# Banded attention and a gated MLP in one kernel: the late attention two units at a time, in thirteen visits instead of thirty-six

## The chip, the cores and the metric

One core of a Trainium2 chip runs one program. The metric is the time of the program on the device in microseconds, the median of several runs. The engines are TensorE (PE; PEld is its weight load), VectorE (DVE), ScalarE (ACT), GpSimd (POOL) and SyncE (SP, which issues most DMAs).

## The reference

Attention over 4 batches and 8 heads of 768 positions with 64 elements each. The positions fall into 24 chunks of 32. A chunk's queries see 8 memory tokens, 16 positions to the left, the chunk itself and 8 positions to the right. The result, 3072 tokens of 512, goes through an RMS norm and a gated MLP with 1536 hidden elements:

```
k_full = concat(mem_k, k[chunk - 16 : chunk + 40]);  v_full likewise
scores = q_c @ k_full.T / 8;  a = exp(scores - max);  a = a / (sum(a) + 1e-9)
x = a @ v_full                               # per chunk and head, then (3072, 512)
xn = x / sqrt(mean(x*x) + 1e-6) * rms_g
g = xn @ w_gate;  out = (silu(g) * (xn @ w_val)) @ w_out
```

## The kernel before, in words

All is fp32. In the MLP each operand is split into a high and a low part, and each product is made of three matmuls (high·high, low·high, high·low: `PASS`).

**Work units.** The tokens fall into 8 blocks of 384. A block's attention is four units, one for each pair of heads, so there are 32 units; units 0 to 7 (blocks 0 and 1) are made early, units 8 to 31 late. A unit goes through these steps: `load_qk` (8 DMA issues, L165 and L167) and `load_v` (a copy of the memory values on ScalarE, L227, and DMAs, L211); `stage_t` (L287 and L292: transposes of q and k on VectorE, with two copies on ScalarE); `stage_s` (L318, s: 12 matmuls, shown as 24); `stage_m` (L330, L336: maximum and subtraction on VectorE) and `stage_e` (L341, exp on ScalarE); `stage_p` (L348, pT: three transposes on TensorE); `stage_c` (L227 and L230: a copy of pT's upper half on ScalarE and of its lower half on VectorE); `stage_o` (L368, o); `stage_r` (L382 to L391: division on VectorE, into x). The late units before share one set of buffers: q and pT in one tile (tag A), k and v in another (tag B), and qn, kn, single too, for the untransposed loads.

**MLP of a block.** For each of 12 slices f of the hidden layer, TensorE makes a gate group pg and a value group pv (L561, 12 matmuls each, PSUM banks "g" and "v"), and an output group po (L599, 9 matmuls) of the slice before; ScalarE and VectorE make hh and hl between them (tanh L568, L572, L575, cast L227, L584). `split_x` between two blocks transposes the normed x (xT, L440) and makes its high and low parts xh, xl (L445, L450). `finish` (from L611, po L627) is the last slice of the last block.

**Order.** Blocks 0 and 1, with the preparation of the weights, stand in the string `ORDER`, a row of tokens, each one step of a unit, of the weights or of the MLP; its instructions are issued in that order. The rest is a loop over seven segments (L857): slices 5 to 11 of block 0, then blocks 2 to 7. In segment n the attention of block n + 2 is made in visits, as long as there is one. A segment has two gaps for each slice, numbered from 0: an even one behind pg, an odd one behind pv and ahead of po. A visit at a gap puts its steps there (`visit`, L870). TensorE's instructions keep the program's order (`on_pe`); those of the other engines are placed by a scheduler, with the visits at a higher priority. `attn_visits` (L688) has six visits of a block on TensorE: s | pT s | pT s o | pT s o | pT o | o, where each piece is of another unit, and a seventh for the norm (`stage_n`: squares on ScalarE, L398; the root on GpSimd, L412; the scaling, L419 and L421). The gaps are `FIRST` in the first segment and are spread out evenly in the others.

Of the kernel before, what the change touches and what calls it, by code (L numbers as in the profile page):

```python
# [19 lines left out]
CH = 32  # L20
# [3 lines left out]
P = 128  # L24
# [43 lines left out]
def tile_kernel(ctx: ExitStack, tc: tile.TileContext, q, k, v, mem_k, mem_v,  # L68
# [48 lines left out]
    NE = NG * 2  # L117
    late_kv = {}
    KW, VW = (NC + 1) * KC, NJ * 2 * (D + 1)

    def late_attention():

        t = p1.tile([P, NKT * HT], F32, name="qp", tag="A")
        n = NC * 2 * CH
        qbs[0] = t[:, 0:n].rearrange("p (c s q) -> p c s q", c=NC, s=2)
        pts[0] = t[:, n:].rearrange("p (i a s q) -> p i a s q", i=NT, a=4, s=2)
        nc.vector.memset(t, 0.0)
        t = p1.tile([P, KW + VW], F32, name="kv", tag="B")
        late_kv["kw"] = t[:, 0:KW].rearrange("p (c k) -> p c k", k=KC)
        late_kv["vw"] = t[:, KW:].rearrange("p (j h d) -> p j h d", j=NJ, h=2)  # L130
    units = [(b, hf, g) for b in range(B) for hf in range(2) for g in range(NG)]
    st = {}

    def which(u):

        return 1 + u % 2 if u < NE else 0

    def unit_tile(u, shape, tag, n):

        if u < NE:  # L140
            return early.tile(shape, F32, name=f"{tag}{u}", tag=f"{tag}{u % n}")
        if tag in late_kv:
            return late_kv[tag]
        return p1.tile(shape, F32, name=f"{tag}{u}", tag=tag)
# [123 lines left out]
    def stage_q0(u, e="a"):  # L268
        d = st[u]
        qb = qbs[which(u)]  # L270
# [12 lines left out]
    def stage_ta(u):  # L283
        d = st[u]
        qb = qbs[which(u)]
        for hh in range(2):
            nc.vector.transpose(out=qb[64 * hh:64 * hh + 64, :, hh, :], in_=d["q"][64 * hh:64 * hh + 64])  # L287
# [21 lines left out]
    def stage_s(u):  # L309
        d = st[u]  # L310
        qb = qbs[which(u)]
        s = psum_a(f"s{u}")
# [29 lines left out]

    def stage_p(u):
        d = st[u]
        t = psum_a(f"pT{u}") if u >= NG else psum_m("o0", f"pT{u}")
        pe = d["p"].rearrange("p j k -> p (j k)")
        for i in range(NT):
            on_pe(nc.tensor.transpose(out=t[:, i * P:(i + 1) * P], in_=pe[:, i * P:(i + 1) * P], identity=ident))  # L348
        d["t"] = t
# [5 lines left out]
    def stage_ch(u, hh, e):  # L355
        r = slice(64 * hh, 64 * hh + 64)
        t4 = st[u]["t"][:, 0:HT].rearrange("p (i a q) -> p i a q", i=NT, q=CH)
        copy(e, pts[which(u)][r, :, :, hh, :], t4[r])

    def stage_o(u):  # L360
        d = st[u]
        pt = pts[which(u)]
        o = psum_a(f"o{u}") if u >= NG else psum_m(f"o{1 + u % 2}", f"o{u}")
        for i in range(NT):
# [44 lines left out]
    def stage_ny(ss):  # L409
        sr = p2.tile([P, NT], F32, name="sr", tag="sr")  # L410
        nc.vector.scalar_tensor_tensor(out=sr, in0=ss[:, 0], scalar=DM * 1e-6, in1=ss[:, 1], op0=ALU.add, op1=ALU.add)
# [275 lines left out]

    def attn_visits(blk, x):  # L688


        us = list(range(blk * NG, (blk + 1) * NG))
        for n in range(NG + 2):
            with tc.high_priority():
                if 1 <= n <= NG:
                    stage_p(us[n - 1])
                if n < NG:
                    u = us[n]
                    stage_s(u)
# [12 lines left out]
            if n < NG and u + 2 < len(units):
                load_qk(u + 2)
            yield
        with tc.high_priority():
            stage_n(x)
        yield

# [74 lines left out]
    def tok_o(n):  # L792
# [62 lines left out]
    xs = xs01[0]  # L855
    nxt = 2
    for sg, (blk, f0) in enumerate(segments):  # L857
        po = [psm_o(i) for i in range(NT)] if sg else sp["po", 0]
        todo = iter(())
        if nxt < NBLK:  # L860
            x = new_x()
            todo = attn_visits(nxt, x)
            nxt += 1
        last = sg == len(segments) - 1
        gaps = 2 * (NF - f0)
        when = [n * (gaps - GAPS) // (NG + 1) for n in range(NG + 2)] + [gaps - GAPS + 1]
        if sg == 0:
            when = FIRST
# [60 lines left out]
```

## Time and profile before

| what | value |
|---|---|
| time, median of 3 runs | 732.41 us (731.84 to 733.12) |
| span of the profiled execution | 729.8 us |
| instructions | 13052 |
| TensorE busy | 715.1 us, 5136 instructions |
| VectorE, ScalarE, GpSimd busy | 380.0, 287.8, 36.4 us |
| moved by DMA | 50.20 MB |

The span is the time of the profiled execution from its first to its last instruction; the program's time is some 2.6 us longer than this span. A row of the timeline gives the start in the span, the duration, engine, line and operation, what is written and read, the shapes and the count, and in brackets how long the engine was idle just ahead and which instruction ended that. Rows of the same kind in succession are drawn together (x24); their duration is that of all together.

### The profile page before, as it was taken

The page shows a single profiled execution, that of the slowest core. Times are in us where ns is not written, and L with a number is a line of the kernel's source. Part 1 is how long each engine was busy: PE and PEld are TensorE (multiplying, and loading weights), DVE is VectorE, ACT ScalarE, POOL GpSimd, SP SyncE. Part 2 cuts the span into 40 slices and gives each one's busy share as a digit, 9 for nine tenths or more (in the row PEclk, how much of TensorE's full clock was granted, in tenths as well). Part 3 has the DMA queues.
Part 4 walks back from the last instruction along what each step waited for, and adds up shares of the span by engine and source line. Part 5 has one row for each costly group of instructions (what it writes and reads, how often), then busy time and mean ns, then how long its engine had stood idle before and what let it go on. Part 6 is the DMA issues. An engine that isn't in the chain of part 4 may idle for free.

```text
span 729.8 us, 13052 instructions
## 1 busy us (share of the span) xinstructions
PE 715.1 (98%) x5136; PEld 656.6 (90%) x5136; DVE 380.0 (52%) x725; ACT 287.8 (39%) x600; POOL 36.4 (5%) x143
## 2 busy tenths in 40 slices
PE   8889999999999999999999999999999999999997
PEld 7778999999989999899999999989998999999996
DVE  4888999865645443444535353445434543332222
ACT  4899676643452323422333232432234222341112
POOL 3300000001000000000000000000000000000000
PEclk8999999999999999999999999999999999999999
DMA  8994563414412320122212123021311210010001
GB/s 173 203 259 141 173 202 116 132 37 102 85 37 68 55 50 22 62 46 42 43 38 66 23 45 61 20 66 31 66 29 34 64 32 20 20 44 0 1 1 43
DMA packets 143173, 50.20 MB, mean 69 GB/s; under 512 B 126984, under 2 KB 134536, under 8 KB 143112
## 3 DMA queue, kind: packets, MB, share of 16 engines
q1 hardware_dynamic: 139832, 44.49, 26.6%
q10 hardware_dynamic: 3280, 4.88, 1.8%
q8 instruction: 40, 0.66, 0.4%
q14 instruction: 21, 0.17, 0.1%
HBM read 43.06 MB, written 6.29 MB: 68 GB/s over the span
## 4 chain that ended last, share of the span: by engine, by line
PE 92%; ACT 3%; DMA 3%; DVE 1%; issue 0%; POOL 0%; ACTq 0%; SPq 0%; POOLq 0%
PE pv L561 28%; PE po L599 28%; PE pg L561 27%; PE s L318 3%; PE o L368 3%; PE xT L440 1%; PE pT L348 1%; DMA ws<-in_moe_w_val_dram 1%; DMA memV<-in_mem_v_dram 1%; DMA vw<-in_v_dram 1%; ACT junk L398 0%; ACT ws L508 0%; ACT pt L227 0%; DMA kv<-in_v_dram 0%; ACT qb L227 0%
## 5 line engine op out<-in xcount | busy, mean ns | idle before, releaser
L561 PE MATMUL pv<-xh,wh_v 128*128 128x384 f32 x384 | 132.8, 346 | 0.0
L561 PE MATMUL pg<-xh,wh_g 128*128 128x384 f32 x384 | 129.7, 338 | 0.7 <-DVE t L572 0.7
L561 PE MATMUL pv<-xh,wl_v 128*128 128x384 f32 x384 | 129.5, 337 | 0.6 <-DVE wl_v L532 0.6
L561 PE MATMUL pg<-xh,wl_g 128*128 128x384 f32 x384 | 129.5, 337 | 0.0
L561 PE MATMUL pg<-xl,wh_g 128*128 128x384 f32 x384 | 129.3, 337 | 0.0
L561 PE MATMUL pv<-xl,wh_v 128*128 128x384 f32 x384 | 129.3, 337 | 0.0
L572 DVE SCALAR_TENSOR_TENSOR t<-t,pg 128x384 f32<-128x384 f32 x96 | 53.1, 553 | 138.6 <-ACT t L568 138.5
L227 ACT CAST hh<-t 128x384 fp32r<-128x384 f32 x95 | 48.7, 512 | 174.9 <-PE po L599 165.3
L599 PE MATMUL po<-wh_o,hh 128*128 128x512 f32 x285 | 113.8, 399 | 0.3
L599 PE MATMUL po<-wh_o,hl 128*128 128x512 f32 x285 | 113.1, 397 | 0.0
L599 PE MATMUL po<-wl_o,hh 128*128 128x512 f32 x285 | 112.1, 393 | 0.0
L584 DVE TENSOR_TENSOR hl<-t,hh 128x384 fp32r<-128x384 f32 x95 | 52.9, 557 | 100.7 <-ACT hh L227 95.7
L568 ACT ACTIVATE t<-pg 128x384 f32<-128x384 f32 x96 | 47.2, 492 | 135.9 <-PE pg L561 130.8
L575 DVE TENSOR_TENSOR t<-t,pv 128x384 f32<-128x384 f32 x95 | 52.5, 552 | 64.9 <-PE pv L561 64.4
L561 PEld LDWEIGHTS pg<-xh,wh_g 128*128 128x128 f32 x384 | 72.1, 188 | 4.4 <-DVE t L572 0.9
L561 PEld LDWEIGHTS pg<-xl,wh_g 128*128 128x128 f32 x384 | 72.1, 188 | 3.6
L561 PEld LDWEIGHTS pv<-xh,wh_v 128*128 128x128 f32 x384 | 72.1, 188 | 2.4
L561 PEld LDWEIGHTS pv<-xh,wl_v 128*128 128x128 f32 x384 | 72.2, 188 | 0.9 <-DVE wl_v L532 0.9
L561 PEld LDWEIGHTS pv<-xl,wh_v 128*128 128x128 f32 x384 | 72.2, 188 | 0.3
L561 PEld LDWEIGHTS pg<-xh,wl_g 128*128 128x128 f32 x384 | 72.1, 188 | 0.0
L599 PEld LDWEIGHTS po<-wh_o,hl 128*128 128x128 f32 x285 | 53.5, 188 | 14.1 <-DVE hl L584 1.8
L599 PEld LDWEIGHTS po<-wh_o,hh 128*128 128x128 f32 x285 | 53.5, 188 | 10.0 <-ACT hh L227 1.7
(112 smaller groups left out, 772.9 us busy)
## 6 DMA issues: line engine op xcount, KB each, us to landing
kn<-in_k_dram SPq DMA_DIRECT2D x96, 52.0 KB
qn<-in_q_dram SPq DMA_DIRECT2D x96, 48.0 KB
out_dram<-ob ACTq DMA_DIRECT2D x18, 256.0 KB
ws<-in_moe_w_gate_dram SPq DMA_DIRECT2D x4, 1024.0 KB
ws<-in_moe_w_val_dram SPq DMA_DIRECT2D x4, 1024.0 KB
ws<-in_moe_w_out_dram SPq DMA_DIRECT2D x4, 1024.0 KB
kv<-in_v_dram SPq DMA_DIRECT2D x48, 84.0 KB
kv<-in_v_dram SPq DMA_DIRECT2D x48, 70.0 KB
```

The lines of the kernel that those rows point to most:

```text
L227: return nc.scalar.copy(out, in_)
L318: on_pe(nc.tensor.matmul(s[64 * par:64 * par + 64, o:o + KC], lhsT=qb[:, c].rearrange("p s q -> p (s q)"), rhs=kw[:, c], start=True, stop= ...
L348: on_pe(nc.tensor.transpose(out=t[:, i * P:(i + 1) * P], in_=pe[:, i * P:(i + 1) * P], identity=ident))
L368: on_pe(nc.tensor.matmul(o[64 * par:64 * par + 64, c0:c0 + D + 1], lhsT=pt[:, i, 2 * par + hh].rearrange("p c q -> p (c q)"), rhs=d["v"][: ...
L440: on_pe(nc.tensor.transpose(out=t[:, i * P:(i + 1) * P], in_=tiles[i][:, kt * P:(kt + 1) * P], identity=ident))
L561: on_pe(nc.tensor.matmul(ps[:, 0:HT], lhsT=weight(a, n, f, kt), rhs=xs[c][:, kt], start=cnt == 0, stop=cnt == 3 * NKT - 1))
L568: nc.scalar.activation(t, g, AF.Tanh, scale=0.5)
L572: nc.vector.scalar_tensor_tensor(out=t, in0=t, scalar=1.0, in1=g, op0=ALU.add, op1=ALU.mult)
L575: nc.vector.tensor_tensor(out=t, in0=t, in1=vv, op=ALU.mult)
L584: nc.vector.tensor_tensor(out=hl, in0=t, in1=hh.bitcast(F32), op=ALU.subtract)
L599: on_pe(nc.tensor.matmul(po[i], lhsT=h[a][:, i * P:(i + 1) * P], rhs=weight(c, "o", f), start=f == 0 and n == 0, stop=f == NF - 1 and n == 2))
```

## The change

**Late attention in pairs.** `late_steps` takes the place of `attn_visits`. It goes over the twelve pairs of late units in one generator for all blocks. A full visit on TensorE is pT pT of the pair before, s s of this pair, o o of the pair before, and ends with "v". There are 13: one with s s alone, eleven full ones, and the last in two parts, pT pT ("p") and o o. A table `VISITS` says for each segment at which gap which step comes: "v", "n" (the norm), and "t" (the transposes of q and k of the pair's second unit; those of its first come with the visit). Transposes of a pair are put behind the last VectorE instruction issued so far (`behind_last`). In a pair both units' V are loaded in the visit of their s.

**Banks.** In a visit the first pT goes into the gate bank "g", the second o into the value bank "v" (not in the last visit), and the rest into the three banks of `psa`.

**Buffers.** Each unit of a pair has its own set: the odd ones the old ones (A and B), the even ones new tiles in the space that the staging of the weights leaves (tags "qb", "ws" and "wy"). qn and kn stay single, so the loads of a unit start when those of the unit before are transposed.

**The first late unit in `ORDER`.** New tokens R0 to R4: R0 loads q and k of unit 8, R1 makes its buffers (a memset of qb1), R2 transposes it, R3 makes pt1 (a memset), R4 loads its V and q and k of unit 9.

**The end.** In `finish` hh and hl take tags A and B instead of "hh" and "hl".

**Places.** The tiles `zero` and `first` move to the early pool, `ss` and `sr` to the single one. The lines before and after in what follows: pT L348 and L377, s L318 and L346, o L368 and L398, pg and pv L561 and L591, po L599 and L629, xT L440 and L470, the transposes L287/L292 and L315/L320, copies L227/L230 and L255/L258.

```diff
+VISITS = (((1, "v"), (4, "t"), (5, "v"), (8, "t"), (11, "v"), (12, "n")),
+          ((2, "t"), (5, "v"), (8, "t"), (17, "v"), (18, "n"), (20, "t")),
+          ((5, "v"), (8, "t"), (17, "v"), (18, "n"), (20, "t")),
+          ((5, "v"), (8, "t"), (17, "p"), (18, "v"), (19, "n")))
...
-j13 F g14 k13a I l13 Ha L Z J o13 f h14 F I v14 i14 Ha L g15 j14 Z J k14a f l14 F v15 h15 I i15 Ha
-g16 j15 J L f F o14 I Ha L v16 k15a l15 h16 o15 i16 j16
+j13 F g14 k13a I l13 Ha L Z J o13 f h14 F I v14 i14 Ha L g15 j14 Z R0 J k14a f l14 F v15 h15 I i15 R1 Ha
+g16 j15 J L R2 R4 f F o14 I Ha R3 L v16 k15a l15 h16 o15 i16 j16
...
-    def stage_p(u):
+    def stage_p(u, tag=None):
         d = st[u]
-        t = psum_a(f"pT{u}") if u >= NG else psum_m("o0", f"pT{u}")
+        tag = tag or (None if u >= NG else "o0")
+        t = psum_m(tag, f"pT{u}") if tag else psum_a(f"pT{u}")
...
-        hh = p1.tile([P, HT], F32R, name="hh", tag="hh")
-        hl = p1.tile([P, HT], F32R, name="hl", tag="hl")
+        hh = p1.tile([P, HT], F32R, name="hh", tag="A")
+        hl = p1.tile([P, HT], F32R, name="hl", tag="B")
...
+    def behind_last(u):
+        done = next(i for i in reversed(nc.cur_bb.bb.instructions) if i.engine == nc.vector.engine)
+        with tc.issue_after(done):
+            stage_t(u)
+
+    def late_steps():
+
+
+        pairs = [(u, u + 1) for u in range(NE, len(units), 2)]
+        for n in range(len(pairs) + 1):
+            old = pairs[n - 1] if n else ()
+            cur = pairs[n] if n < len(pairs) else ()
+            new = pairs[n + 1] if n + 1 < len(pairs) else ()
+            for u in old[0:1]:
+                if u % NG == 0:
+                    late_x["x"] = new_x()
+            x = late_x.get("x")
             with tc.high_priority():
-                if 1 <= n <= NG:
-                    stage_p(us[n - 1])
-                if n < NG:
-                    u = us[n]
+                for i, u in enumerate(old):
+                    stage_p(u, None if i else "g")
+                for u in old:
+                    stage_c(u)
+            if not cur:
+                yield "p"
+            with tc.high_priority():
+                for u in cur:
                     stage_s(u)
...
+                for u in cur:
                     stage_m(u)
+                for u in cur:
                     stage_e(u)
...
+                for i, u in enumerate(old):
+                    stage_o(u, "v" if cur and i else None)
+                for u in old:
+                    stage_r(u, x)
+                for u in new[0:1]:
+                    behind_last(u)
+            for u in new[0:1]:
+                load_qk(u + 1)
+            for u in cur if n else ():
+                load_v(u)
+            yield "v"
+            if n and n % 2 == 0:
+                with tc.high_priority():
+                    stage_n(x)
+                yield "n"
+            if new:
+                with tc.high_priority():
+                    behind_last(new[1])
+                if n + 2 < len(pairs):
+                    load_qk(pairs[n + 2][0])
+            yield "t"
...
+        if n == 0:
+            load_qk(NE)
+        if n == 1:
+            late_buffers(1)
+        if n == 2:
+            stage_t(NE)
+        if n == 3:
+            late_pt()
+        if n == 4:
+            load_v(NE)
+            load_qk(NE + 1)
```

TensorE in a visit of block 4 (units 16 to 18), before: the end of a gate group, one piece of each kind, and the start of the value group.

```order
L561 MATMUL pg_3689<-xh_3391,wl_g2_94 128x384
L348 MATMUL pT17_3702<-ident_99,pe17_3593 128x128 x3
L318 MATMUL s18_3706<-kv_1946,qp_1944 64x64 x12
L368 MATMUL o16_3719<-kv_1946,qp_1944 64x65 x12
L561 MATMUL pv_3768<-xh_3391,wh_v2_95 128x384
```

After, units 16 to 19 in a full visit between a value group and an output group:

```order
L591 MATMUL pv_3634<-xh_3488,wl_v1_90 128x384
L377 MATMUL pT16_3648<-ident_99,kv1_1882 128x128 x3
L377 MATMUL pT17_3652<-ident_99,pe17_3246 128x128 x3
L346 MATMUL s18_3660<-kv1_1882,qb1_1880 64x64 x12
L346 MATMUL s19_3673<-kv0_1978,qp0_1976 64x64 x12
L398 MATMUL o16_3695<-kv1_1882,pt1_1942 64x65 x12
L398 MATMUL o17_3708<-kv0_1978,qp0_1976 64x65 x12
L629 MATMUL po0_3541<-wh_o1_91,hh_3617 128x512
```

The visit has moved from behind pg to behind pv and holds two units of each kind, next to each other.

VectorE in the first segment, before, around the copy of the first late pT (pT8; qn and kn are the loaded q and k, t the gate's product):

```order
L584 TENSOR_TENSOR hl_2065<-t_2059,hh_2063 128x384
L292 STREAM_TRANSPOSE kv_1946<-kn9_1965 128x13x32
L336 TENSOR_TENSOR pe8_2038<-s8_2023,mx8_2036 128x384
L572 SCALAR_TENSOR_TENSOR t_2144<-t_2144,pg_2067 128x384
L575 TENSOR_TENSOR t_2144<-t_2144,pv_2080 128x384
L230 COPY qp_1944<-pT8_2093 64x12x32
```

After, at the same copy:

```order
L614 TENSOR_TENSOR hl_2154<-t_2148,hh_2152 128x384
L315 STREAM_TRANSPOSE qp0_1976<-qn11_2095 64x12x32 x2
L320 STREAM_TRANSPOSE kv0_1978<-kn11_2096 128x13x32
L602 SCALAR_TENSOR_TENSOR t_2322<-t_2322,pg_2156 128x384
L605 TENSOR_TENSOR t_2322<-t_2322,pv_2187 128x384
L258 COPY pt1_1942<-pT8_2201 64x12x32
L258 COPY qp0_1976<-pT9_2205 64x12x32
L358 TENSOR_REDUCE mx10_2239<-s10_2213 128x6
```

By then units 9 to 11 are transposed where it was unit 9 alone, and the transposes of unit 11 stand directly ahead of the read of pg.

ScalarE in the first segment, before, around the norm of block 2 (memV are the memory values, junk and ss the squares, sr the root), up to the first xh:

```order
L568 ACTIVATE t_2516<-pg_2442 128x384
L398 ACTIVATE junk_2493,ss_2492<-x_1978 128x384 x3
L227 COPY kv_1946<-memV_102 128x12x64
L398 ACTIVATE junk_2497,ss_2492<-x_1978 128x128 x3
L419 ACTIVATE x_1978<-x_1978,sr_2501 128x512
L227 CAST hh_2520<-t_2516 128x384
L568 ACTIVATE t_2550<-pg_2524 128x384
L445 ACTIVATE xh_2558<-xT0_2560,rg_100 128x384
```

After:

```order
L255 COPY kv0_1978<-memV_102 128x12x64
L428 ACTIVATE junk_2602,ss_2601<-x_2200 128x384 x2
L428 ACTIVATE junk_2606,ss_2601<-x_2200 128x128
L255 CAST hh_2584<-t_2580 128x384
L428 ACTIVATE junk_2602,ss_2601<-x_2200 128x384
L428 ACTIVATE junk_2606,ss_2601<-x_2200 128x128
L328 COPY kv1_1882<-kv1_1882 128x12x16
L329 COPY kv1_1882<-kv1_1882 128x11x8
L428 ACTIVATE junk_2606,ss_2601<-x_2200 128x128
L598 ACTIVATE t_2629<-pg_2588 128x384
L449 ACTIVATE x_2200<-x_2200,sr_2610 128x512
L475 ACTIVATE xh_2637<-xT0_2639,rg_100 128x384
```

The squares now stand behind both copies of memory values and among copies of the next block's k; fewer MLP steps lie between the scaling and the first xh.

More of the change, by code (lines that the diff above doesn't have):

```diff
@@ L117, in tile_kernel, with late_buffers, late_pt, late_views @@
     NE = NG * 2
-    late_kv = {}
+    late = {}
     KW, VW = (NC + 1) * KC, NJ * 2 * (D + 1)
[L121 to L130, printed above, removed]
+    NQ = NC * 2 * CH
+    def late_buffers(i):
+        if i:
+            late["qb", 1] = p1.tile([P, NQ], F32, name="qb1", tag="qb")
+            nc.vector.memset(late["qb", 1], 0.0)
+        else:
+            t = p1.tile([P, NKT * HT], F32, name="qp0", tag="A")
+            late["qb", 0], late["pt", 0] = t[:, 0:NQ], t[:, NQ:]
+            nc.vector.memset(t, 0.0)
+        t = p1.tile([P, KW + VW + i * NJ * KC], F32, name=f"kv{i}", tag=("B", "ws")[i])
+        late["kw", i] = t[:, 0:KW].rearrange("p (c k) -> p c k", k=KC)
+        late["vw", i] = t[:, KW:KW + VW].rearrange("p (j h d) -> p j h d", j=NJ, h=2)
+        if i:
+            late["pe", i] = t[:, KW + VW:].rearrange("p (j k) -> p j k", k=KC)
+        else:
+            late_views("pt", i)
+        late_views("qb", i)
+    def late_pt():
+        late["pt", 1] = p1.tile([P, NQ], F32, name="pt1", tag="wy")
+        nc.vector.memset(late["pt", 1], 0.0)
+        late_views("pt", 1)
+    def late_views(n, i):
+        if n == "qb":
+            late[n, i] = late[n, i].rearrange("p (c s q) -> p c s q", c=NC, s=2)
+        else:
+            late[n, i] = late[n, i].rearrange("p (i a s q) -> p i a s q", i=NT, a=4, s=2)
     units = [(b, hf, g) for b in range(B) for hf in range(2) for g in range(NG)]
     st = {}
-    def which(u):
-        return 1 + u % 2 if u < NE else 0
+    def qb_of(u):
+        return qbs[1 + u % 2] if u < NE else late["qb", 1 - u % 2]
+    def pt_of(u):
+        return pts[1 + u % 2] if u < NE else late["pt", 1 - u % 2]
     def unit_tile(u, shape, tag, n):
@@ L269, in stage_q0 @@
         d = st[u]
-        qb = qbs[which(u)]
+        qb = qb_of(u)
         q4 = split4(d["tq"], HT)
@@ L284, in stage_ta @@
         d = st[u]
-        qb = qbs[which(u)]
+        qb = qb_of(u)
         for hh in range(2):
@@ L310, in stage_s @@
         d = st[u]
-        qb = qbs[which(u)]
+        qb = qb_of(u)
         s = psum_a(f"s{u}")
@@ L357, in stage_ch, with stage_o @@
         t4 = st[u]["t"][:, 0:HT].rearrange("p (i a q) -> p i a q", i=NT, q=CH)
-        copy(e, pts[which(u)][r, :, :, hh, :], t4[r])
-    def stage_o(u):
+        copy(e, pt_of(u)[r, :, :, hh, :], t4[r])
+    def stage_o(u, tag=None):
         d = st[u]
-        pt = pts[which(u)]
-        o = psum_a(f"o{u}") if u >= NG else psum_m(f"o{1 + u % 2}", f"o{u}")
+        pt = pt_of(u)
+        tag = tag or (None if u >= NG else f"o{1 + u % 2}")
+        o = psum_m(tag, f"o{u}") if tag else psum_a(f"o{u}")
         for i in range(NT):
@@ L711, in attn_visits @@
[L711 to L716, printed above, removed]
+                for i, u in enumerate(old):
[8 more added lines that the diff above has]
+                load_v(u)
@@ L855, in tile_kernel @@
     xs = xs01[0]
-    nxt = 2
+    todo = late_steps()
     for sg, (blk, f0) in enumerate(segments):
         po = [psm_o(i) for i in range(NT)] if sg else sp["po", 0]
[L859 to L863, printed above, removed]
         last = sg == len(segments) - 1
[L865 to L868, printed above, removed]
+        steps = {} if last else dict(VISITS[min(sg, 2) + (sg == len(segments) - 2)])
         def visit(gap):
-            for _ in range(when.count(gap)):
-                next(todo, None)
+            if gap in steps and next(todo, None) not in (steps[gap], None):
+                raise AssertionError(gap)
         for f in range(f0, NF):
```

44 lines of the change are left out of this document (14 added, 30 removed).

## The prediction

> **What bounds the kernel now.** I read the totals first, then the busy table by stretches, then the timeline of TensorE around single visits, then the waits that end idle time on TensorE. The totals and the page's row on TensorE:
>
> ```profile
> span 729.8 us, 13052 instructions
> PE 715.1 (98%) x5136; PEld 656.6 (90%) x5136; DVE 380.0 (52%) x725; ACT 287.8 (39%) x600; POOL 36.4 (5%) x143
> ```
>
> TensorE is busy 715.1 of 729.8 us, every other engine half as long or less. So the change can gain where TensorE does less or waits less, and lose where it waits anew. The next rows put a segment with attention beside the last one, which has none; both run from the first gate matmul to the point where the last 10 of 12 output groups lie behind (12 pg, 12 pv and 10 po groups). Columns: stretch, us, busy time of PE, PEld, DVE, ACT and POOL, granted TensorE clock, DMA share, GB/s.
>
> ```profile
> 563.81:644.13 80.32, 80.32 (x584) 74.60 (x583) 34.21 (x70) 22.98 (x55) 2.66 (x10) 1.00 0.15 34
> 650.07:721.20 71.13, 71.13 (x379) 67.17 (x378) 18.89 (x34) 12.24 (x25) 0.00 (x0) 1.00 0.03 12
> ```
>
> TensorE has no gap in either (80.32 of 80.32, 71.13 of 71.13). The attention of one block of four units therefore costs 80.32 − 71.13 = 9.19 us of TensorE, and six late blocks cost 55.1 us. The 205 instructions more are, but for one, 4 × (3 pT + 24 s + 24 o). The instructions stay the same; only what the switches between kinds of work cost can fall.
>
> **Part by part. 1: the pieces merge (−8.1).** TensorE's timeline of a visit with s alone, of one with three pieces, and the row of nine transposes of x (start, us, instruction, shapes, count):
>
> ```profile
> 220.70 0.34 PE L561 MATMUL pg<-xh,wl_g 128*128 128x384 f32 x1
> 220.97 0.97 PE L318 MATMUL s<-kv,qp 128*64 128x64 f32 x24
> 221.86 0.45 PE L561 MATMUL pv<-xh,wh_v 128*128 128x384 f32 x1
> ...
> 246.18 0.34 PE L561 MATMUL pg<-xh,wl_g 128*128 128x384 f32 x1
> 246.36 0.49 PE L348 MATMUL pT<-ident,pe 128*128 128x128 f32 x3
> 246.78 0.97 PE L318 MATMUL s<-kv,qp 128*64 128x64 f32 x24
> 247.53 0.92 PE L368 MATMUL o<-kv,qp 128*64 128x65 f32 x24
> 248.38 0.44 PE L561 MATMUL pv<-xh,wh_v 128*128 128x384 f32 x1
> 248.66 0.34 PE L561 MATMUL pv<-xl,wh_v 128*128 128x384 f32 x1
> ...
> 644.13 1.14 PE L440 MATMUL xT<-ident,x 128*128 128x128 f32 x9
> ```
>
> From start to start, pT takes 0.42, s before an o 0.75, s before a large matmul 0.89, o 0.85. The first large matmul behind a visit takes 0.28 (248.38 to 248.66) where one beside its like takes 0.18 (246.18 to 246.36): 0.10. An s that follows a large matmul pays about 0.09 at its entry (0.27 from 220.70 to 220.97), and I take 0.07 for an o alone. Before, the six visits of a block are s | pT s | pT s o | pT s o | pT o | o: 0.98 + 1.31 + 2.02 + 2.02 + 1.27 + 0.92, and six times 0.10, is 9.1: it accounts for the 9.19.
>
> After, TensorE has thirteen visits: one s s, eleven of pT pT s s o o, and the last as pT pT and o o one gap apart. Three transposes more behind the first three cost 3 × 0.108 (nine span 1.14 and three 0.49: 0.65 for six), so pT pT 0.74. Two s cost 1.49 (2 × 0.745). For the first o of two no row shows the switch; its 24 matmuls leave 0.85 less the 0.14 by which s before a large matmul exceeds s before an o, so 0.71, and o o takes 1.55. With 0.10 behind it a full visit is 3.88; eleven are 42.7. The first visit is 0.09 + 1.64 + 0.10 = 1.8, the last 0.74 and 1.75. Together 47.0 against 55.1: **−8.1**. The bounds: if a switch to the second piece of a kind cost as much as to another kind, a visit would be 2 × 0.42 + 2 × 0.75 + 2 × 0.85 + 0.10 = 4.14, 2.9 more in eleven; below, the pair of transposes could be 0.66 and the second s 0.70, 1.4 less.
>
> **2: the first block's wait goes (−1.15).**
>
> ```profile
> 203.22 1.26 PE L368 MATMUL o<-kv,qp 128*64 128x65 f32 x24 [0.80 <-DMA kv<-in_v_dram]
> 204.42 0.44 PE L561 MATMUL pv<-xh,wh_v 128*128 128x384 f32 x1
> ```
>
> The last o of block 2 waits 0.80 for its values and then runs 1.20 instead of 0.85. After, the values of a pair are loaded in the visit that computes its s, and are used in the next visit, four gaps or more away, some 3 us each (the segment of 80.32 us has 24). Nothing is late next at this place; what is late a little behind it is step 4.
>
> **3: the end (−0.4).**
>
> ```profile
> 721.20 0.40 PE L599 MATMUL po<-wh_o,hh 128*128 128x512 f32 x1
> ...
> 723.06 0.40 PE L599 MATMUL po<-wh_o,hl 128*128 128x512 f32 x1
> 723.61 0.50 PE L627 MATMUL po<-wh_o,hh 128*128 128x512 f32 x1 [0.15 <-ACT hh L621]
> 723.26 0.70 ACT L621 CAST hh<-t 128x128 fp32r<-128x128 f32 x3 [3.46 <-PE po L599]
> ```
>
> The last hh is cast only when the po group ahead has read the old hh (3.46 of waiting), so the last group starts 0.55 behind the matmul ahead instead of (723.06 − 721.20) / 8 = 0.23, and its first matmul is 0.1 longer. With hh and hl in buffers that are free by then the cast runs beside that po group: −0.4.
>
> **4: the norm of block 2 gets tight (+1.4).** The rows of that norm before:
>
> ```profile
> 202.85 0.49 ACT L398 ACTIVATE junk<-x 128x384 f32<-128x384 f32 x1
> 203.48 0.49 ACT L398 ACTIVATE junk<-x 128x384 f32<-128x384 f32 x1
> 204.66 0.82 ACT L227 COPY kv<-memV 128x768 f32<-128x768 f32 x1
> 205.55 0.28 ACT L398 ACTIVATE junk<-x 128x128 f32<-128x128 f32 x1
> 205.99 0.28 ACT L398 ACTIVATE junk<-x 128x128 f32<-128x128 f32 x1
> 207.28 0.15 DVE L411 SCALAR_TENSOR_TENSOR sr<-ss 128x3 f32<-128x3 f32 x1
> 208.40 0.72 ACT L419 ACTIVATE x<-x,sr 128x512 f32<-128x512 f32 x1 [1.57 <-POOL sr L412]
> ```
>
> Before, the squares of three of the four head pairs stood ahead of the last o. After, the visit at gap 11 brings the last two units of the block, and all six squares stand behind it on ScalarE, behind two copies of pT, two exps and two copies of memV. From the visit's start T0: o o ends at 3.9, the second memV copy (0.82) at about 5.4; the squares take 3 × 0.63 + 3 × 0.44 = 3.2, and a hh cast and two kv copies of 0.95 in all stand among them: 9.5. Then 0.1, 1.12 to the root (207.28 to 208.40) and 0.9 for scaling three tiles on two engines: 11.6. TensorE reaches xT after the visit (3.9), a po (9 × 0.23), pg and pv (12 × 0.174 each, from the two stretches' 71.13): 10.2. It waits 11.6 − 10.2 = **1.4**, bounds 0.9 and 1.9 by half a us in the order on ScalarE. The other five norms have five gaps or more of TensorE work behind them, some 15 us, and cost nothing; without that cover each would cost the like.
>
> **5: transposes on VectorE that wait for a DMA (+0.2).** Each pair has two transposes on VectorE (q and k), and the second unit's load can only start when the first's is transposed. Around gap 5 of block 0 those of unit 11 stand ahead of t<-t,pg (L572), which frees the gate bank that the next pT, lent that bank, now needs: the first pT and all of TensorE behind it would wait.
>
> ```profile
> 173.04 0.47 SPq L167 DMA_DIRECT2D kn<-in_k_dram  x1
> 176.59 0.61 DVE L292 STREAM_TRANSPOSE kv<-kn 128x416 f32<-128x416 f32 x1 [0.57 <-DMA kn<-in_k_dram]
> 188.66 0.47 SPq L167 DMA_DIRECT2D kn<-in_k_dram  x1
> 191.40 0.61 DVE L292 STREAM_TRANSPOSE kv<-kn 128x416 f32<-128x416 f32 x1
> ```
>
> From the last issue of a load to its transpose lie 3.55 us where it waited and at most 2.74 where it did not. The loads of units 9, 10 and 11 hang on each other through one buffer, so the difference of 0.8 counts up to three times: a wait of 2.3, or none. I take 0.2, near the unwaited row, since of these two landings one only was waited for. The Trainium skill's "DMA: Bandwidth & Descriptors" (Anatomy of one DMA) puts the fixed part of a transfer at about 2 us, under both rows; by it the wait would be nothing and the time 0.2 lower, and no run here shows the fixed part alone.
>
> **6: block 0 and 1's end (+0.15).** Into the row of tokens go two memsets and a unit's transposes on VectorE:
>
> ```profile
> 1.57 0.70 DVE L656 MEMSET qb<- 128x768 f32 x1
> 156.88 0.56 DVE L584 TENSOR_TENSOR hl<-t,hh 128x384 fp32r<-128x384 f32 x1 [0.27 <-ACT hh L227]
> 158.91 0.40 PE L599 MATMUL po<-wh_o,hl 128*128 128x512 f32 x1
> 248.26 1.17 DVE L287 STREAM_TRANSPOSE qp<-qn 64x384 f32<-64x384 f32 x2
> ```
>
> The hl shown ends at 157.44 and is first read at 158.91: 1.5 of room. Ahead of it now stand 0.70 + 1.17 + 0.61 = 2.5 of new work, of which I estimate that 1 us falls into VectorE's idle time: it then starts at 158.4, ends at 158.96 and is read some 0.1 later. **+0.15**, bounds 0 and 0.5 (no idle time at all would cost 1 us, but 0.27 of it stands in the row itself and more ahead). The same memset and transposes leave the place behind, where TensorE did not wait for them.
>
> **What stays covered.** In a full visit VectorE has the product with pv and two copies of pT (0.56 each by the row below), to end 1.8 behind T0; the first o takes the PSUM bank of the second pT at T0 + 0.74 + 1.49 = 2.23. This cover is 0.4 us thin, and rival 2 is its loss.
>
> ```profile
> 233.71 0.56 DVE L230 COPY qp<-pT 64x384 f32<-64x384 f32 x1
> ```
>
> **Sum.** −8.1 − 1.15 − 0.4 + 1.4 + 0.2 + 0.15 = −7.9: a span of 721.9 from 729.8. The median of 732.41 lies 2.6 above the profiled span, the part outside it: **724.5 us**.
>
> **Rivals.** (1) The forecast, 0.72, alone 722.0 to 727.5. (2) The copies come late at the first o: with one further VectorE row of 0.56 ahead the 0.4 turns into 0.2 of waiting, with two into 0.75; eleven visits make 2.2 to 8.3, so 726.7 to 732.8. Against it stands the order, which puts only the product ahead. 0.12. (3) Pairs pay each switch: 727.4 by the bound in part 1. For it speaks that no row shows a pair; against it, that nine transposes keep 0.108. 0.10. (4) Slower: the clock falls in visits made of small matmuls and transposes alone. The stretches near the start:
>
> ```profile
> 11.31 0.94 PE L318 MATMUL s<-kw,qb 128*64 128x64 f32 x24 [2.45 <-POOL kw L221]
> 13.00:19.70 6.70, 6.70 (x57) 5.83 (x57) 3.25 (x7) 4.45 (x11) 0.58 (x3) 0.50 0.88 185
> 19.70:52.00 32.30, 27.62 (x482) 23.90 (x482) 27.09 (x60) 27.82 (x62) 6.28 (x13) 1.00 1.04 228
> ```
>
> Behind a wait of 2.45 in transposes and short matmuls the clock stood at 0.50 for 6.7 us. One such fall costs 6.7 / 2 = 3.4 us; three undo the 7.9 and the result is slower, thirteen cost 44 (768 us). Against it: from 19.70 to 52.00 only small matmuls run, with TensorE 14% idle, at 1.00. "TensorE: Matmul & The Clock Gate" of the Trainium skill (Part 1, and Part 4 on transposes) says the gate falls to half rate after some 3.4 us without activity and that transposes do not count as such; by it a visit, with 0.74 of transposes, stays clear, and the trace's 32 us agree. 0.06. That the change would not do what it says is ruled out by the order of TensorE's instructions.
>
> **Numbers.** A measurement of this kernel can tell about 0.2% (1.5 us) from no change: faster is below 730.9. Rivals 1 and 3 and half of 2 are faster (0.72 + 0.10 + 0.07), 0.04 of rival 2 lies within, the rest and rival 4 make 0.07. The range goes from 722.0 (the low bounds of parts 1 and 4 to 6) to 728.5, with rival 3 and the lower end of 2 in it; about 0.2 of the chance stays outside.
>
> **What would show it.** Right: full visits of 3.9 on TensorE with no wait inside, one wait of 1 to 2 us at xT of block 2, no wait for the values there, and hh at the end cast beside the po group. Wrong: a wait for VectorE or ScalarE at o in every visit (rival 2), s s above 1.6 (3), a granted clock below 1.00 behind 70 us (4), or waits at gate or value groups that I costed at nothing.

## The result, and the profile after

| | before | after |
|---|---|---|
| median of 5 runs | 732.41 us (730.99 to 733.42) | 726.36 us (725.66 to 728.26) |
| span of the profiled execution | 729.8 us | 723.9 us |
| TensorE busy | 715.1 us | 708.6 us |

The ratio is 0.992, 95% interval 0.9906 to 0.9934: 6.05 us faster where 7.9 was forecast, and 726.36 lies in the range of 722.0 to 728.5. One execution of experiment e2 below, the only profiled one of that kernel, ran at a third of the usual pace from end to end and is not read. The first row of nine xT, at the end of block 1's attention, stands at 64.3 to 67.4 us in the profiled executions, whatever the edit, so parts are compared from that row on.

The totals of the page after, and of the waits of TensorE the two of over 0.05 us that lie behind 66 us (us in total, times, longest):

```profile
span 723.9 us, 13126 instructions
PE 708.6 (98%) x5136; PEld 656.0 (91%) x5136; DVE 382.1 (53%) x727; ACT 284.2 (39%) x600; POOL 35.5 (5%) x143
...
PE pT L377 <- DVE t L602: 1.4, 1, 1.4
...
PE xT L470 <- DVE x L451: 0.4, 1, 0.4
```

The wait at o for values is gone. Two have come instead, both in block 0: one at the first late pT (predicted 0.2), one at block 2's xT (predicted 1.4). Everything else of the shortfall must be in busy time.

A full visit on TensorE in the steady state, after:

```profile
405.26 0.49 PE L377 MATMUL pT<-ident,kv 128*128 128x128 f32 x3
405.59 0.49 PE L377 MATMUL pT<-ident,pe 128*128 128x128 f32 x3
406.01 0.97 PE L346 MATMUL s<-kv,qb 128*64 128x64 f32 x24
406.76 0.92 PE L346 MATMUL s<-kv,qp 128*64 128x64 f32 x24
407.46 0.92 PE L398 MATMUL o<-kv,pt 128*64 128x65 f32 x24
408.16 0.92 PE L398 MATMUL o<-kv,qp 128*64 128x65 f32 x24
409.01 0.50 PE L629 MATMUL po<-wh_o,hh 128*128 128x512 f32 x1
409.35 0.39 PE L629 MATMUL po<-wl_o,hh 128*128 128x512 f32 x1
```

pT pT 0.75, s s 1.45, o o 1.55, and 0.11 more at the first po (0.34 instead of 0.23): 3.85, where 3.88 was predicted. The ten visits behind the first agree within 0.01.

The first wait, on VectorE and SyncE and then on TensorE, after:

```profile
174.28 2.57 SPq L195 DMA_DIRECT2D kn<-in_k_dram  x3
...
177.41 0.47 SPq L195 DMA_DIRECT2D kn<-in_k_dram  x1
...
177.05 0.57 DVE L315 STREAM_TRANSPOSE qp<-qn 64x384 f32<-64x384 f32 x1 [1.08 <-DMA qn<-in_q_dram]
178.87 0.58 DVE L315 STREAM_TRANSPOSE qp<-qn 64x384 f32<-64x384 f32 x1 [1.25 <-DMA qn<-in_q_dram]
179.63 0.61 DVE L320 STREAM_TRANSPOSE kv<-kn 128x416 f32<-128x416 f32 x1 [0.18 <-DMA kn<-in_k_dram]
180.17 0.52 DVE L602 SCALAR_TENSOR_TENSOR t<-t,pg 128x384 f32<-128x384 f32 x1
...
180.74 0.55 PE L377 MATMUL pT<-ident,kv 128*128 128x128 f32 x3 [1.44 <-DVE t L602]
```

Unit 11's eight loads are issued one behind the other from 172.79 to 177.88. One of the three in the row of 2.57 takes 1.65 us alone, where the other seven issues take 0.31 to 0.48. The unit's transposes wait three times on VectorE, and t<-t,pg, which could have run, stands behind them.

The second wait, and the end, after:

```profile
212.70 0.17 DVE L441 SCALAR_TENSOR_TENSOR sr<-ss 128x3 f32<-128x3 f32 x1 [0.85 <-ACT junk L428]
213.83 0.88 DVE L451 TENSOR_SCALAR x<-x,sr 128x512 f32<-128x512 f32 x2 [0.20 <-POOL sr L442]
214.37 1.38 PE L470 MATMUL xT<-ident,x 128*128 128x128 f32 x9 [0.43 <-DVE x L451]
215.50 0.48 PE L629 MATMUL po<-wh_o,hh 128*128 128x512 f32 x1
...
717.61 0.40 PE L629 MATMUL po<-wh_o,hl 128*128 128x512 f32 x1
717.84 0.40 PE L657 MATMUL po<-wh_o,hh 128*128 128x512 f32 x1
718.08 0.40 PE L657 MATMUL po<-wl_o,hh 128*128 128x512 f32 x1
```

The norm ends with the visit's start plus 9.1 at sr (9.5 predicted) and TensorE waits 0.43; the nine xT then take 1.13 instead of 0.90, since the last tile is scaled late: 0.66 in all. At the end the last po group follows after 0.23, without a wait.

**What is missing.** A slice of the MLP itself takes longer. Slice 11 of a steady block, from the last po of slice 10 over pg and pv to xT, first before, then after:

```profile
553.48 0.39 PE L599 MATMUL po<-wh_o,hl 128*128 128x512 f32 x1
...
557.87 0.38 PE L440 MATMUL xT<-ident,x 128*128 128x128 f32 x2
```

```profile
550.37 0.39 PE L629 MATMUL po<-wh_o,hl 128*128 128x512 f32 x1
...
554.83 0.38 PE L470 MATMUL xT<-ident,x 128*128 128x128 f32 x2
```

4.39 before, 4.46 after, with the same 24 matmuls, the same shapes and no visit near. Over all segments the matmuls inside a pg or pv group follow each other in 174.5 ns before and 175.5 after (worked out from their starts, without the first and the last of each group); inside a po group it is 232.9 and 233.9. That happens in the last segment too, which has no attention. The question for the experiments was where it comes from.

Table of parts, in us (from the row of nine xT that opens a part to the next; the first part runs from 65 us over the end of blocks 0 and 1 and slices 5 to 11 of block 0). The columns from e1 on belong to the experiments:

| part | before | e1 | e11 | after | e3 | e6 | e5 | e10 |
|---|---|---|---|---|---|---|---|---|
| to block 2 | 147.79 | 148.15 | 147.27 | 149.69 | 148.45 | 148.21 | 149.40 | 147.60 |
| block 2 | 86.26 | 86.50 | 86.08 | 85.30 | 85.29 | 85.18 | 84.85 | 84.85 |
| block 5 | 86.26 | 86.67 | 86.10 | 85.05 | 85.07 | 84.86 | 84.59 | 84.59 |
| block 6 | 86.26 | 86.49 | 86.10 | 83.59 | 83.60 | 83.43 | 83.19 | 83.17 |
| pg, pv inside (ns) | 174.5 | 175.5 | 173.4 | 175.5 | 175.5 | 174.7 | 173.5 | 173.5 |
| median time | 732.4 | 735.5 | 731.0 | 726.4 | 726.1 | 724.3 | 723.2 | 721.9 |

### The profile page after: what moved, and what is told of

It is laid out like the page before. It is cut to its first block, busy times and chain, and to the rows that moved or that the text cites. A ratio compares the mean times of both kernels' runs of the same rounds, so it can differ in the third digit from the quotient of the medians.

```text
span 723.9 us, 13126 instructions
## 1 busy us (share of the span) xinstructions
PE 708.6 (98%) x5136; PEld 656.0 (91%) x5136; DVE 382.1 (53%) x727; ACT 284.2 (39%) x600; POOL 35.5 (5%) x143
## 4 chain that ended last, share of the span: by engine, by line
PE 89%; ACT 4%; DVE 2%; DMA 2%; issue 1%; SPq 1%; POOL 0%; ACTq 0%; DVEq 0%; POOLq 0%
PE po L629 27%; PE pv L591 26%; PE pg L591 26%; PE s L346 3%; PE o L398 2%; PE xT L470 1%; PE pT L377 1%; ACT junk L428 1%; DMA memV<-in_mem_v_dram 1%; ACT pt L255 1%; DMA kv<-in_v_dram 1%; ACT qb L255 0%; ACT wy L539 0%; ACT ws L538 0%; SPq L195 0%
## 5 line engine op out<-in xcount | busy, mean ns | idle before, releaser
L591 PE MATMUL pg<-xh,wh_g 128*128 128x384 f32 x384 | 130.0, 339 | 0.7 <-DVE t L602 0.7
L591 PE MATMUL pv<-xh,wl_v 128*128 128x384 f32 x384 | 129.5, 337 | 0.5 <-DVE wl_v L562 0.5
L591 PE MATMUL pv<-xh,wh_v 128*128 128x384 f32 x384 | 129.7, 338 | 0.0
L591 PE MATMUL pv<-xl,wh_v 128*128 128x384 f32 x384 | 129.6, 337 | 0.0
L591 PE MATMUL pg<-xh,wl_g 128*128 128x384 f32 x384 | 129.5, 337 | 0.0
L591 PE MATMUL pg<-xl,wh_g 128*128 128x384 f32 x384 | 129.4, 337 | 0.0
L255 ACT CAST hh<-t 128x384 fp32r<-128x384 f32 x95 | 48.6, 512 | 201.9 <-PE po L629 177.8
L629 PE MATMUL po<-wh_o,hh 128*128 128x512 f32 x285 | 114.7, 402 | 0.3
L629 PE MATMUL po<-wh_o,hl 128*128 128x512 f32 x285 | 113.1, 397 | 0.0
L629 PE MATMUL po<-wl_o,hh 128*128 128x512 f32 x285 | 112.3, 394 | 0.0
L591 PEld LDWEIGHTS pg<-xh,wh_g 128*128 128x128 f32 x384 | 72.0, 188 | 4.6 <-DVE t L602 0.9
L591 PEld LDWEIGHTS pg<-xl,wh_g 128*128 128x128 f32 x384 | 72.1, 188 | 3.5
L591 PEld LDWEIGHTS pv<-xh,wl_v 128*128 128x128 f32 x384 | 72.0, 188 | 0.8 <-DVE wl_v L562 0.8
L591 PEld LDWEIGHTS pv<-xh,wh_v 128*128 128x128 f32 x384 | 72.1, 188 | 0.4
L591 PEld LDWEIGHTS pv<-xl,wh_v 128*128 128x128 f32 x384 | 72.1, 188 | 0.3
L591 PEld LDWEIGHTS pg<-xh,wl_g 128*128 128x128 f32 x384 | 72.0, 188 | 0.0
L629 PEld LDWEIGHTS po<-wh_o,hl 128*128 128x128 f32 x285 | 53.5, 188 | 14.4 <-DVE hl L614 2.0
L629 PEld LDWEIGHTS po<-wh_o,hh 128*128 128x128 f32 x285 | 53.5, 188 | 10.5 <-ACT hh L255 1.7
```

The source lines that it names most:

```text
L255: return nc.scalar.copy(out, in_)
L591: on_pe(nc.tensor.matmul(ps[:, 0:HT], lhsT=weight(a, n, f, kt), rhs=xs[c][:, kt], start=cnt == 0, stop=cnt == 3 * NKT - 1))
L629: on_pe(nc.tensor.matmul(po[i], lhsT=h[a][:, i * P:(i + 1) * P], rhs=weight(c, "o", f), start=f == 0 and n == 0, stop=f == NF - 1 and n == 2))
```

## The experiments

Each is set against the kernel before, whose median beside them was 732.5 to 732.6 us.

**e1: only the places of four small tiles, on the kernel before.**

```diff
-    zero = const.tile([P, 64], F32, name="zero")
+    zero = early.tile([P, 64], F32, name="zero")
...
-        ss = p2.tile([P, 2, NT], F32, name="ss", tag="ss")
+        ss = p1.tile([P, 2, NT], F32, name="ss", tag="ss")
```

(and `first` and `sr` likewise)

> The kernel before with nothing changed but where four small tiles lie (zero and first in the early pool, ss and sr in the single one), as the change has it. The order on all engines is that of before; x, xh, xl lie 288 bytes lower, hh and hl 288. Theory A (the places of the operands slow the MLP's matmuls): the inner spacing of pg and pv goes from 174.5 to about 175.5 ns in each segment, some 0.35 us for each of six segments and 0.7 up to the first of them, together +2.5 to +3: about 735. Theory B (long runs of the MLP without a visit slow them): 732.4, and 174.5 ns stays.

735.52 us (733.33 to 736.69), ratio 1.0031 (1.0019 to 1.0043). The same slice 11:

```profile
557.14 0.39 PE L599 MATMUL po<-wh_o,hl 128*128 128x512 f32 x1
...
561.60 0.38 PE L440 MATMUL xT<-ident,x 128*128 128x128 f32 x2
```

4.46 as after, and 175.5 ns on average: every engine has the work of before in the same order, and only addresses differ. Theory A holds, B falls. In the traces it costs 0.36 in the first part and 0.23 to 0.42 in each of the blocks, 2.2 us from 67.11 us to the end; the medians differ by 2.9.

**e2: x 32 bytes higher, on the kernel after.**

```diff
+    p1.tile([P, 2, NT], F32, name="ss0", tag="ss")
     x = new_x()
```

> The kernel after with one small tile (ss) allocated ahead of x, so that x, xh, xl and the two buffers behind them lie 32 bytes higher, at 96 in 128 as before; weights, hh and hl stay, and so does the order on all engines. Theory A: slices 0, 1 and 4 go back from 174.7 to about 173.4 ns, slices 5 to 9 stay at 176, slices 10 and 11 (176) are open: 0.1 to 0.25 us for each segment, so 724.6 to 725.7 against 726.4 after. Theory B: 726.4 and the same spacing.

725.95 us (725.33 to 727.0 in four executions) against 732.6, ratio 0.9909 (0.9891 to 0.9926). By its times no gain over 726.36 shows, and the spacing in e2 itself stays unknown. e6 holds the same edit on top of e3's, and its trace has the spacing.

**e3: the gate operation ahead of unit 11's transposes, on the kernel after.**

```diff
+            t = None
+            if sg == 0 and f == f0 + 2:
+                with tc.high_priority():
+                    t = silu_a(g)
+                    silu_b(t, g)
             visit(2 * (f - f0))
...
-                prev = moe_h(g, vv)
+                prev = moe_h(g, vv, t)
```

> The kernel after with one VectorE instruction moved: in slice 7 of block 0, t<-t,pg stands ahead of unit 11's transposes instead of behind them. Theory: the wait of 1.44 us at the first late pT is that of the gate bank, held up by transposes that wait for a load; it goes, and 0 to 0.3 comes back at s, which needs those transposes: 725.0 to 725.3. Rival (the wait only moves to s or o): 726 or more, with the wait shown there.

726.1 us (725.61 to 726.71), ratio 0.991 (0.9893 to 0.9926). In its trace the visit:

```profile
181.49 0.49 PE L377 MATMUL pT<-ident,pe 128*128 128x128 f32 x3
181.91 0.97 PE L346 MATMUL s<-kv,qb 128*64 128x64 f32 x24
183.04 0.94 PE L346 MATMUL s<-kv,qp 128*64 128x64 f32 x24 [0.17 <-issue]
```

The wait of 1.44 at pT is gone, and 0.17 stands at the second s, which costs 0.4, since s now takes 1.13 instead of 0.75. The load is as late as after: its last issue ends 1.5 us ahead of the first pT here (179.68 and 181.16), and 1.4 ahead of that pT's turn after (177.88 and 179.30). The first part is 1.24 shorter than after. The medians differ by 0.3 only, less than expected: the lateness of the load differs between executions, as the trace of e5 shows (below), and so few runs of the two kernels don't tell 1 us.

**e4: hh and hl of the last slice in their old buffers, on the kernel after.**

```diff
-        hh = p1.tile([P, HT], F32R, name="hh", tag="A")
+        hh = p1.tile([P, HT], F32R, name="hh", tag="hh")
```

(and hl)

> The kernel after with hh and hl of the last slice in their old buffers. Theory: the last group starts 0.3 later behind the po group and its first matmul takes 0.1 longer, as before: +0.4, 726.8. Rival (hidden by the DVE product or the cast anyway): below +0.1.

728.05 us (726.29 to 730.29), ratio 0.9937 (0.9919 to 0.9955), and in the trace:

```profile
719.54 0.39 PE L629 MATMUL po<-wh_o,hl 128*128 128x512 f32 x1
720.09 0.50 PE L657 MATMUL po<-wh_o,hh 128*128 128x512 f32 x1 [0.16 <-ACT hh L651]
720.43 0.40 PE L657 MATMUL po<-wl_o,hh 128*128 128x512 f32 x1
```

The 0.55 and 0.34 of before are back; from block 7's first xT to the last matmul it takes 82.09 instead of 81.68: 0.41. The median rose by 1.7, more than the edit explains. Of the 2.4 by which the profiled spans differ, 1.96 lie ahead of the first row of xT, far from the edit.

**e5 and e6: the places again, with e3's edit.** e5 allocates kn ahead of x, e6 ss:

```diff
+    p1.tile([P, NC + 1, CH], F32, name="kn0", tag="kn")
     x = new_x()
```

> The kernel with the gate operation ahead of unit 11's transposes, and the tile kn allocated ahead of x, which moves x, xh, xl (and hh, hl, t) up by 1664 bytes, to 192 in 256; the order on all engines stays. Theory A, refined (the pace of pg and pv follows weight address minus xh address, in 256): fast at differences 32 and 192, slow at 128 and 160 in the traces of before and after. Here slices 0 to 4 have 192 and 5 to 9 have 32, so 173.2 ns for ten of twelve slices, 0.5 to 0.8 us less for each segment than after: 721 to 723. If the places matter but not by this difference, any pace from 173 to 177. Theory B: 726.1, as with the gate operation moved alone.

> The kernel with the gate operation ahead of unit 11's transposes, and xh and xl 32 bytes higher, at 96 in 256 as before. Differences: 32 (slices 0 to 4), 128 (5 to 9), 96 (10 and 11). Theory A, refined: 173.4, 176 and open: 725.0 to 725.8 against 726.1. Theory B: 726.1, 175.5 ns on average in all segments.

e5: 723.18 us (722.67 to 723.89), ratio 0.987 (0.9846 to 0.9894). e6: 724.34 us (724.09 to 724.49), ratio 0.9883 (0.9863 to 0.9903). Both have e3's order on all engines and differ from it in addresses alone. Slice 11 in e5:

```profile
548.31 0.39 PE L630 MATMUL po<-wh_o,hl 128*128 128x512 f32 x1
...
552.71 0.49 PE L470 MATMUL xT<-ident,x 128*128 128x128 f32 x3
```

4.40. The groups of slices 0 to 9 average 172.8 to 174.7 ns in e5, in e6 those of slices 0 to 4 173.3 to 175.3 and of 5 to 9 175.3 to 176.3: the refined theory names which slices are slow, with exceptions among the gate groups (three of e6 at 174.7 to 175.3 and two of e5 at 174.7, which it calls fast). e5 ended 0.2 above the range expected, e6 0.7 below its own. The first part of e5 (149.40) is hardly better than after's, because its second s waits in that execution:

```profile
180.67 0.61 DVE L320 STREAM_TRANSPOSE kv<-kn 128x416 f32<-128x416 f32 x1
...
181.92 0.94 PE L346 MATMUL s<-kv,qp 128*64 128x64 f32 x24 [1.41 <-ACT kv L329]
```

Here the last issue of unit 11's load ends at 179.00, 0.2 behind the start of the first pT at 178.81. So e3's edit removes the queueing, not the late load: where unit 11 lands later still, s waits for what pT waited for.

**e7: no banks lent, on the kernel after.**

```diff
-                    stage_p(u, None if i else "g")
+                    stage_p(u)
...
-                    stage_o(u, "v" if cur and i else None)
+                    stage_o(u)
```

> The kernel after with pT, s and o of a visit all in the three banks of the ring, none lent; the order on all engines stays. Theory: the second s waits for the copies of the first pT (about 0.1), the first o for those of the second pT, and the second o for the read of the first s on VectorE, which ends 0.3 to 0.8 behind its turn: +0.4 to +0.9 for each of eleven visits, 731 to 736. Rival (TensorE's own work covers the copies): below 728.

732.41 us (730.81 to 736.5), ratio 1.0001 (0.9985 to 1.0017): the whole gain is gone. A visit on TensorE:

```profile
411.53 0.49 PE L377 MATMUL pT<-ident,kv 128*128 128x128 f32 x3
411.85 0.49 PE L377 MATMUL pT<-ident,pe 128*128 128x128 f32 x3
412.27 0.97 PE L346 MATMUL s<-kv,qb 128*64 128x64 f32 x24
413.26 0.94 PE L346 MATMUL s<-kv,qp 128*64 128x64 f32 x24
413.99 0.92 PE L398 MATMUL o<-kv,pt 128*64 128x65 f32 x24
414.99 0.93 PE L398 MATMUL o<-kv,qp 128*64 128x65 f32 x24
415.84 0.50 PE L629 MATMUL po<-wh_o,hh 128*128 128x512 f32 x1
```

4.31 instead of 3.74: the second s starts 0.24 late (behind the copy of the first pT) and the second o 0.30 (behind VectorE's last read of the first s). Hardly any of it shows as a gap between matmuls, so the waits are read from the starts. Ten of the eleven visits are 0.57 longer; the first, at gap 5, has 2.36 of waiting at its second s, with unit 11's late load behind it.

**e8: VectorE's copy of the first pT twice, on the kernel after.**

```diff
                 for u in old:
                     stage_c(u)
+                    if cur and u % 2 == 0:
+                        stage_ch(u, 1, "d")
```

> The kernel after with VectorE's copy of the first pT of each full visit made twice: 0.5 us more ahead of the second pT's copy, whose end frees the bank that the first o takes. If the cover there is the 0.4 us of the prediction, each of eleven visits waits 0.1: 727.5. If it is the 0.13 us that the trace of after shows in one visit, each waits 0.35 to 0.4: 730.3 to 730.8. If the cover is larger than either, 726.4.

733.39 us (732.04 to 734.63), ratio 1.0008 (0.9997 to 1.0019). The scheduler put the repeated copy third, so that the first o waits for its own operand:

```profile
410.87 0.56 DVE L258 COPY pt<-pT 64x384 f32<-64x384 f32 x1 [0.28 <-ACT pt L255]
411.35 0.55 DVE L258 COPY qp<-pT 64x384 f32<-64x384 f32 x1
411.82 0.56 DVE L258 COPY pt<-pT 64x384 f32<-64x384 f32 x1
...
412.59 0.93 PE L398 MATMUL o<-kv,pt 128*64 128x65 f32 x24 [0.34 <-issue]
```

The copy ends at 412.38 and o starts 0.21 later; s s takes 2.01 instead of 1.45. A visit is 4.31, 0.57 longer: 6.3 us in eleven, above both of my figures (the medians differ by 7.0). The wait is for the operand, and not for the bank that I meant to test. Nothing of the 0.5 us was hidden, so VectorE's copies in the kernel after have nearly no cover at the first o.

**e9 and e10: other gaps in the first segment, on e5.** e9 has the third visit at gap 9 instead of 11 and the norm at 10, e10 the second visit at gap 7 instead of 5:

```diff
-VISITS = (((1, "v"), (4, "t"), (5, "v"), (8, "t"), (11, "v"), (12, "n")),
+VISITS = (((1, "v"), (6, "t"), (7, "v"), (10, "t"), (11, "v"), (12, "n")),
```

> The kernel of e5 (gate operation first, x at 192 in 256) with block 2's last visit two gaps earlier, at gap 9 instead of 11, and its norm at gap 10. Theory: the wait of xT for block 2's norm (0.46, and 0.24 more in the longer row of transposes) goes, as the norm has 6 us more of TensorE ahead of xT: 722.5 against 723.2. The transposes of unit 13 then stand closer to their use at gap 9; if they are late, a wait of up to 1.5 appears at that s and the time is 723 to 724.

> The kernel of e5 with block 2's second visit two gaps later, at gap 7 instead of 5 (unit 11 transposed at gap 6, unit 13 at gap 10, the gate operation ahead of both). Theory: unit 11's load then has 6 us more and the wait at the second s (1.41 in e5's trace, 0.17 in e6's) goes in every run; the norm's wait stays: 721.8 to 723.0 against 723.2. Rival: units 12 and 13 come as late to gap 11 as unit 11 did to gap 5, and the wait is found there instead: 723.2 or more.

e9: 722.33 us (721.69 to 723.2), ratio 0.9853 (0.9834 to 0.9873). The wait at xT is gone; one of 0.62 is at the second s of gap 5, the late load of e5. e10: 721.86 us (720.95 to 722.38), ratio 0.9849 (0.9831 to 0.9866), the fastest kernel of the study. Its waits from 66 us on are two of 0.17 and 0.18 at the second s of the visits at gaps 7 and 11, the second of which is

```profile
202.81 0.97 PE L346 MATMUL s<-kv,qb 128*64 128x64 f32 x24
203.96 0.94 PE L346 MATMUL s<-kv,qp 128*64 128x64 f32 x24 [0.18 <-issue]
```

and costs 0.4 (1.15 instead of 0.75). I had expected the norm's wait to stay in e10; it went too, and the traces of e5 and e10 show why. In e10 sr starts 8.92 us behind that visit's first pT (202.07 and 210.99) instead of 9.10, because the last square no longer stands behind two copies of k on ScalarE. TensorE, held up by 0.4 at s, comes to xT 10.72 behind it instead of 10.30. So part of the norm's wait now stands at s, and the nine xT still take 1.13. e9 and e10 don't differ by more than their spread.

**e11: 96 unused bytes ahead of x, on the kernel before.**

```diff
+    p1.tile([P, 24], F32, name="pad", tag="pad")
     x = new_x()
```

> The kernel before with an unused tile of 96 bytes ahead of x, which moves x, xh, xl to 192 in 256 (and hh, hl, t and the weights of slices 10 and 11 by the same 96); the order on all engines is that of before. Weight minus xh is then 192, 32 and 192. Theory A, refined: pg and pv at 173.3 instead of 174.5 ns in all segments, 0.3 to 0.4 us for each segment and 0.7 up to the first: 729.5 to 730.3 against 732.5. Rival (the pace gained in e5 belongs to the paired visits): 732.5.

731.03 us (729.28 to 732.01), ratio 0.9973 (0.996 to 0.9987): the pace of e5 (173.4 ns, 173.5 in e5) without paired visits. The time gained is less than I expected, since a block gains 0.17 of the 0.3 to 0.4: po got slower, 234.2 ns instead of 232.9 on average, and takes a part back.

## Why the prediction was right, and where it was off

Parts from 65 us to the end: 664.75 before (729.8 − 65.05), 659.23 after (723.9 − 64.67), 5.5 less. Its terms against the forecast:

| term | forecast | found | from |
|---|---|---|---|
| 1 pieces merge | −8.1 | −8.6 | eleven visits of 3.85, first 1.8, last 0.66 and 1.74: 46.5 of 55.1 |
| 2 wait for values | −1.15 | −1.15 | no such wait after |
| 3 end | −0.4 | −0.4 | e4: 0.41 |
| 4 norm | +1.4 | +0.66 | 0.43 and 0.23 in the rows of xT |
| 5 transposes | +0.2 | +1.5 | 1.44, and e3 |
| 6 end of blocks 0 and 1 | +0.15 | +0.1 | first late s 102.21 behind xT after, 102.12 in e1 |
| the MLP's own pace | none | +2.2 | e1 |
| sum | −7.9 | −5.7 | −5.5 measured |

Without the row on the pace the found terms make −7.9 too, and that is luck: 1 and 4 came out 1.2 lower than forecast, and 5 came out 1.3 higher. That the time lies in the range is luck in part as well, since the range was made wide for pairs that don't merge and for late copies, and it was the MLP's pace and part 5 that used it up.

The mechanism of part 1 was right: visits merged as worked out, rival 3 (no merging) fell with s s at 1.45, and without the lent banks the kernel is as slow as before (e7). Rival 4 fell as well. In the busy table after, a stretch with a full visit at 490.3 us:

```profile
490.00:512.00 22.00, 22.00 (x199) 20.52 (x198) 12.83 (x27) 7.28 (x16) 0.87 (x4) 1.00 0.37 69
```

The granted clock is 1.00, as in the whole execution after from 20 us on, with 3.74 us of small work alone in that visit. "TensorE: Matmul & The Clock Gate" of the Trainium skill (Part 1) asks for some 3.4 us without activity for a fall, and by this trace a visit is no such stretch.

The step that failed is the sentence "The instructions stay the same; only what the switches between kinds of work cost can fall". It took the pace of a matmul as fixed by its shape. The change moved zero, first, ss and sr, and with them x, xh and xl by 288 bytes, which I listed under places and costed at nothing without a row for it. e1 shows 2.2 us of it with no other edit, e5 and e6 that it can be had back, and e11 that the kernel before could gain by places too.

The second is the size of part 5. The bounds, 0 and 2.3, held 1.44; the value near the lower one was a guess from two landings. What the runs show is a chain: a unit's load starts only behind the transposes of the one before, and its eight issues follow each other on SyncE, 3.9 us in the shortest loads and 5.1 here; from the last issue to its transpose it is 2.2 (177.41 to 179.63). The last agrees with the some 2 us that the Trainium skill gives in "DMA: Bandwidth & Descriptors" (Anatomy of one DMA), there for transfers that GpSimd issues, while SyncE issues these. My conclusion from it was wrong: the landing isn't late, the chain of issues is. With 3.9 us of issuing the same rows would leave a wait of some 0.25 us by my estimate, near the 0.2 forecast; the rest is the one issue of 1.65. In all nine traces with pairs (after, e3 to e10) one issue of unit 11's load takes 0.9 to 1.8 us, in the trace before none of that load's takes over 0.5, though another unit's has one of 1.63 at 312.40. What holds it up is open.

Part 4 was too large by half: the squares ended 0.4 earlier than I laid them, TensorE came to xT 0.14 later (10.34 behind the visit's start), and the first xT didn't have to wait until all three tiles were scaled. Rival 2 didn't come about, but by less than I said. I gave its cover as 0.4 us, from copies of 0.56 one behind the other. In the trace after, VectorE's copy of the first pT begins 0.28 later, behind ScalarE's copy of the same pT, and the last copy ends 0.13 ahead of the first o:

```profile
406.30 0.56 DVE L258 COPY pt<-pT 64x384 f32<-64x384 f32 x1 [0.28 <-ACT pt L255]
406.78 0.55 DVE L258 COPY qp<-pT 64x384 f32<-64x384 f32 x1
```

e8 shows what that is worth: 0.5 us more there is paid in full.

The 2.6 us between span and median, which the forecast calls the part outside the span, are not all outside it: the execution profiled after took 725.66 us with a span of 723.9, 1.8 more. If it is the same before, as I take it, the execution profiled there was 0.8 faster than the median. After it is 2.5 by the same reckoning, so in the difference it cancels to 0.1.

## What to carry to other kernels

Where one engine is busy all the time and its instructions stay the same, price the switches between kinds of work, count them before and after, and then ask separately whether the pace of the bulk stays: a change that reorders the allocation of tiles can move it, and the last segment, which holds no attention, is where that can be read. An operation that frees a buffer for the bound engine should not stand in an in-order queue behind one that waits for a load. A thin cover is measured by doubling the work that it hides.

## What the hardware showed that I had not expected

- The pace of fp32 matmuls (128x384, weights 128x128) depends on where their operands lie: 173.1 to 176.8 ns by slice in kernels that differ in addresses alone (e1 and before; e3, e5 and e6). In these runs it went with the address of the weights less that of xh, in 256 bytes (addresses of the program's allocation; the traces hold none): fast at 0, 32 and 192, slow at 128 and 160, mixed at 64 and 96. This rule was made from before and after and named most slices of e5, e6 and e11; other functions of the addresses aren't excluded, and its cause is open.
- po (128x512) follows the places too, and not in the same way: 232.9 ns before, 234.2 in e1 and e11, 233.9 after, 234.9 in e5 and e6.
- A short wait costs TensorE more than its gap: 0.17 of idle time at the second s is 0.4 from start to start, and 0.34 at o in e8 is 0.56. That the overlap of the two pieces' ends is lost would explain it; no run tests that.
- Issues of one kind on SyncE differ: of the eight of unit 11's load after, seven take 0.31 to 0.48 us and one 1.65.
